# Row numbers carried in the sorted rows instead of looked up by table products: a recurrence and a hash-routed mixture of experts on one core

## The chip, the cores and the metric

The kernel runs on one core of a Trainium2 chip. The metric is the device time of one execution in microseconds. Three timed executions of the kernel before took 664.62, 650.76 and 662.44 us; their median, 662.44 us, is the time before. The profile page and the trace come from a further execution, with the profiler, which took 499.46 us. Times within the kernel are read from that execution, and the median of the timed executions is what is predicted.

The engines are called TensorE (PE in the profile; PEld is its loading of weights), VectorE (DVE), ScalarE (ACT), GpSimd (POOL) and SyncE (SP). An entry such as SPq is the queue of an engine's sequencer, here one that issues transfers.

## The reference

Two stages follow one another: a gated recurrence over the sequence and a mixture of experts in which each token goes to the one expert that a hash of its token number names.

```python
batch, seq, d_model = (4, 5056, 256)          # x, f_logit: f32
N, D, E, F = (20224, 256, 8, 1024)            # experts' weights w1 [E, D, F], w2 [E, F, D]: f32

# recurrence
sig = 1.0 / (1.0 + np.exp(-f_logit))
f = lower_bound[None, None, :] + (1.0 - lower_bound[None, None, :]) * sig
i = 1.0 - f
for t in range(S):
    h = f[:, t] * h + i[:, t] * x[:, t]
    y[:, t] = h

# experts, on y as rows [N, D]
expert_idx = token_ids * np.int64(2654435761) % np.int64(E)
for e in range(E):
    mask = expert_idx == e
    xe = x[mask]
    h = np.maximum(xe @ w1[e], 0.0)
    out[mask] = h @ w2[e]
```

The multiplier leaves the remainder 1 when divided by 8, so the expert is the low three bits of the token number. The kernel takes these and sorts by them.

## The kernel before

The sequence is cut into 25 blocks of 64 to 256 steps, each for all four batches; a "group" is 32 steps of four batches, so 128 tokens, and there are 158 of them. All work is cut into tasks, and a packed list (`ORDER`) fixes the order in which the engines get them.

A block is loaded, transposed so that time runs along the free axis, put through the sigmoid and the gate (on ScalarE or VectorE, as the order says), scanned by VectorE, and transposed back into rows. In the first seven blocks TensorE transposes; in the others VectorE does.

Each token gets a place: its rank within its expert, found with running sums and small matrix products. GpSimd then writes a group's 128 rows of y to their places in a sorted array in HBM, with one indirect transfer a group:

```python
srt = dram.tile([E * CAP, D], BF16, name="srt")          # 8 experts x 21 tiles x 128 rows
...
def scatter_rows(k, m, ybuf):
    bi = nc.gpsimd.indirect_dma_start(
        out=srt[:], out_offset=bass.IndirectOffsetOnAxis(ap=pos_i[:, G0[k] + m:G0[k] + m + 1], axis=0),
        in_=T["yT", k][:, m, :], in_offset=None, bounds_check=E * CAP - 1, oob_is_err=False,
    )
```

In seven blocks (`FS`), four of the eight groups go another way. They are sorted by expert on the chip with one-hot matrices and matrix products, written to a scratch array, and moved as one segment of 104 rows for each expert:

```python
def onehot(g=g):
    for c in range(4):
        nc.vector.tensor_scalar(oneh[:, c, :], iotf[:], qf[:, g, c:c + 1], None, op0=ALU.is_equal)
def sort(v, k=k, g=g):
    ...
    nc.tensor.matmul(t[:, j, :], lhsT=oneh[:, c, (2 * v + j) * P:(2 * v + j + 1) * P], rhs=T["yT", k][:, 4 + c, :], ...)
def put(g=g, queue=queue):
    queue.dma_start(scr[g % 3][:4 * P, :]..., T["sb", g]...)
def move(h, k=k, g=g, queue=queue):
    for e in range(4 * h, 4 * h + 4):
        bi = queue.dma_start(srt[bass.ds(T["reg", g][E + e], SEG), :], scr[g % 3][bass.ds(T["reg", g][e], SEG), :])
```

A tile of 128 sorted rows (there are 21 for each of the 8 experts, 168 in all) can be used when all blocks that may reach it have been written. It is read transposed, multiplied by w1, passed through Relu, and multiplied by w2. Its rows go out to their tokens' places by an indirect transfer:

```python
def read(j=j, e=e):
    xe = mp.tile([P, 2, P], BF16, name="xe", bufs=8)
    r0 = e * CAP + j * P
    bi = nc.sync.dma_start_transpose(xe[:], srt[r0:r0 + P, :])
def up(j=j, e=e):
    for f in range(FF):                                   # FF = 8
        for h in range(2):
            nc.tensor.matmul(hp[:, f, :], lhsT=w1_sb[e][:, h, f * P:(f + 1) * P], rhs=xe[:, h, :], ...)
def relu(eng, j=j, e=e):                                  # ScalarE or VectorE
    ...
def down(j=j, e=e, n=n, h=h):
    for f in range(FF):
        nc.tensor.matmul(op[:, h, :], lhsT=T["hT", j, e][:, f, :], rhs=w2_sb[e][:, f, :], ...)
def rows(j=j, e=e, n=n, h=h):
    bi = nc.gpsimd.indirect_dma_start(out=out, out_offset=bass.IndirectOffsetOnAxis(ap=row_i[:, c:c + 1], axis=0), ...)
```

For the last step the kernel must know which token lies in each sorted row (`row_i`). It finds out by products, block by block: one-hots of a token's place within its tile (A) are multiplied by one-hots of its tile, scaled by the two halves of its row number (BP), and summed into a table:

```python
nc.vector.tensor_tensor(A[:, c0:c1, :], iota_lo[...], lo_h[...], op=ALU.is_equal)
nc.vector.tensor_tensor(hi, iota_hi[...], hi_h[...], op=ALU.is_equal)
nc.vector.tensor_tensor(BP[:, c0:c1, 0, :W], hi, v1[...], op=ALU.mult)
nc.vector.tensor_tensor(hi, hi, v2[...], op=ALU.mult)
...
nc.tensor.matmul(tp[:, :, :W], lhsT=A[:, c, :], rhs=BP[:, c, :, :W], ...)
...
nc.vector.tensor_tensor(t, t, T["tp", k][:, :, :W], op=ALU.add)
```

The experts' weights are loaded as f32 on SyncE's queue into the buffers of x and f, and cast to bf16 by ScalarE or VectorE:

```python
nc.sync.dma_start(o.rearrange("k (h f) -> k h f", h=2), moe_w1[e].rearrange("(s h k) f -> k s h f", s=2, h=2))
...
if eng == "ACT":
    nc.scalar.copy(o, i_)
else:
    nc.vector.tensor_copy(o, i_)
```

A flag, computed from the data, leads to a second path for inputs whose tokens are spread too unevenly; the trace doesn't enter it.

Of the kernel before, what the change touches and what calls it, by code (L numbers as in the profile page):

```python
# [11 lines left out]
FP32 = mybir.dt.float32  # L12
BF16 = mybir.dt.bfloat16
FP16 = mybir.dt.float16
I32 = mybir.dt.int32
# [20 lines left out]
RANGES = [(0, 6), (6, GA), (GA, MID), (MID, NG)]  # L36
FILL = (9, 12)
FB = {GA: [9, 10, 11], MID: [13, 15, 17, 19]}
FS = [k for a in (GA, MID) for k in FB[a]]
GF = len(FS)  # L40
FA = ()
SEG = 104
XF = 3
OFF, TABD = 20.0, 25.0
W0, W1 = -70.0, 6.0
# [4 lines left out]
    "jrsgQ8_Q5CFiayEC?J+qP}nww06Q&U<6qwr$(CZCkrPQ5D9d;jAx<&ib(ttUnvTMzMj6u^4PH10z^8Glq?1;cTc`#A2~HEQJ}w5;J9nu#_ePi^+x"  # L50
    "=W8$*WY#Iy93}($Z=Ga&hfh}d8#b%4yc(aKuV-rjyGo7Vl6U`D9ku_zLSSquE5u3$kvQ;br+rnm><!mL}%qFu_EWJr>uCc9b8=GS?noMS{*=|;w5"
    "ZlM*u{9<eTWjXC?B)#H&knGgY=_Bg*0C&XI9tzlnxyQ4-^C8GgX}bG!LphgEQdL4j+k5QEW6Imv7=@;Yi91S^X3?9#s0B{tT{W*E|`1lE-"
    "T9}s+KH1tH3V%OFjv^Xr{6&DyQN661(anoAPEao5F50!7nq(ulZ-}zPau{u@@{JTfl0vimVQ+Z626%?4e1-"
    "DzTSr4?DpUvRdpj+rXZ)jg0YEtS)<PzAzOeH(%LRc7@erCm96aSY_6cRbv=@HyPm(tIvLztWd>tVqMrzb3;95#Ph%}_Qo_~Rn1#d0IIW0po5$Kma"
    "oAg@OLa5bT$o4HOLIvAq(VyH0C#J&Dycj@Sb%w4Owx>3;Cd%dCCexW0s3GVQpD5^M_S}LZQDbKjaK`XKhSGe%t3ZY0U>#7)n3~Qxe*<NW2V`f{(0"
    "7sHb_t%0ds;i&cg@svJ~@@}VlB$o#I4!lUuJPy-V2KBg+f;4yh`lY~d-v4W^Pc2E=I1i2s=Zv*LgvY-"
    "~^=5d3>JZX@J=i_;U{6PjDk0%e(^AthKpg_<9;`3s>9yEkZycEyF>O;YxI4{F9^2|Y&pe)a88bN8Eisyzxyc|!>%LmnXVO|lc^BO#B&=`tAXXwQ%"
    "1pS}^WaCYsCa)OO;w5-?-"
    "V|2wdwvx!3N7KjU(b8<D6Ax}9khbB(2iH)jd(uO4l46HL3e1v6Y>On4S%3I@Gj6A@|$9;6Yt0?K;57RbcHm$Jw!E4c|YDPc<76pw7fBI9&~{AydL"
    "iy^x-{W0B;fG<lUe@AH)Yi4&Dpu^OiwX-imh#R&vdX@`1b#^oG8?YcPvDJ~(L2&+<9^3NOM#yc<tphXk{EcRn;2&OIN;!*~Nep0DHQ`6WJ&&*kTM"  # L60
    "e^|{g@U{Gr4-Y2r`N1&WkT-`(d?FtVm-&cbWUwG;!w10RpeJ7#wB?KVD87MD2|n?w-"
    "0+RTR=zhF0*m?7U{i3B@8|o19{els1XcKEzKo|62l+tQ#((l3d>S9kuLU>x7hW5N!XchfSiY2h<_Gu~m;hV&bZ+6X5BP0<Jt)MQ!FRqqxWTsvhl3"
    "r#FgP9*U}O32;ApTj*cFW7xA<><Cm0Te%?y4w*b@{qkAf%a33uQjtC-"
    "1;1yA`i9tKPJbT|?`^CyDm+`w4)#h>~IK{!l=aqu_@!E9IrGvHn@9!9`7-Vr9j{ouL(6Z{RL*nfNuFfkJXco8gv%p#h|BBI(e{7tYJxSb4h;Z-"
    "1PU&tYr!^>bJEP>a-NRW0G#I-HNTG#=5Ai7uznZ!KECSItM9PA2M32|&Z5nm{~4q{j>NTAIr4#O%q#rwc<h-DMl(|i-O6jLCkZ6y-"
    "f(Qpp3i&3y1BG{cUU95(Lb_28)5p6pW+dd2~!Dg5b?_n=Qvb!L$%_Sn+oAA<qh9i(t?1NMyw=H6xKt8br?!s1h<x`6^VmGXTBK8EN6>UUbQP}3ON"
    "1>P~D$c_UQQ79VCn1?Q1`DBzZ7-^dx50jBD^5Xi+d=$-0ye3rCSI!xa2aNai!c=m+LE?}eF3-"
    "N3Y4~GY&kIvl8EYdJ0uq$_y_+FYT5&E6+ZHNP{?)^x8V-du=k;?K-"
    "S4Vg?IcVl(+ABDVtu@vK4Ixu?^n%3U;=51|MJnG!>`8*#}U`b`^)9v;7EjM1A`T=82i2i?{|~pn>RS8;Os8u6Pb7#Y2dQ4Mk&t*xmN9pVV;SZ5&L"
    "FA<@(Rh9=?@y!C_ZIQtbCzEi#IL5P82cE0!nLqt9C4c`0LKzK?F6=&g#A8bE+j>BwXd;@=>kBEdC1;)fP5N;QU>oCIJfXMhAjIAx=Vmg!<3wzszw"  # L70
    "yx+aPK!Ds0zQTkEFO-uOGIE}<0Dusnu&h4xman>i71!^SBw5O6ArL%AwEXMq?iIz;svqDrpI@{rL}9sKr7`L@e?xRc##u#+TG#@EVU)gL@_~p^%-"
    "!Log|XsGP_481WbVEMJoKJE{W8b3-e+YTyEFe+*lrq;0jwAOJF{nEH>J8mgGed9XHvrVzbDI(Xbv0SroJ4dYd1|h&=eiZxP>pNgOS<+C-"
    "QZ6Jj<@gS+fDJ4Kuoqr_CP*KW5P>@=aImIbgF7Q}tF6xPCA@~1D3`)xj18Y^HKtb&(qQ*4RZF$WgLE_lEe!m?NnE8-"
    "4Y39r~v=C=K%UfZkUosA%`iK^HEYvTz4vJU?C^|1j~!|V2lxMOeFx1ugK#GCe*xGPGtd*Y~gV&B-u)?q|h9h+fu?2k{yecK8TiWYcW^v2fs-sX`V"
    "v8ZW-"
    "4{amtiq8bf5B9n3gl(~m>5RkhrR|1?#7BF}zOa4pfgOp5#djOoMRMJ70QSWm*ijmsf_ddw9Ebr%ku~v=ePwIlC!1Twa{aI|dh9F*VQlwTM3r%50o"
    "erGV=tVKA&lmtyBYXHByzt*JNzkPxKa3948}ixD~`svvL}wiotVn~5f;CR;W!l&yYZOXC6SBqs|dp(I1SUv&teQFbu)1l4#hMwo=fKb`Ytk^3&#a"
    "G0Sn3muCVMR*I`VTUw#p@a5~P$g&5yW#0-wfIhfEDlF8j79D)DTBwT_iToLzA%$Dh06<5YB#f7q%<e`-"
    "A0CtnBaT#WG%W(}Bm+P^d+<<ejs4L;h%bs#AR+HOMgid1%S6yz$l5QjJ!m6&TEbEToWSocRv6rmjcHl}}f!8pz+>M*Cf-"
    "B{+$vW;J=8zBZ5O$Xm_TXMTif6FCtmv}KvzS$~&@rs*>dDgX9L|+B-"  # L80
    "C?ZcYPl>jlYEK|TxE9)Yr6~B+YNS&+;wc|F5(STp)GhE8@ul~)a8_y(7W5%Lq5Vj?j~Nw)^eD<gD3DY4tGP`GyH%d*H_-"
    "f=Ll*uwv=yhp8SoHTFHKLAMVEpAyilKEndMk@*~cX?c_Urf)PV8slWSy_i%uFfdgGs`h<}nOh!_t@Fg~tgIrtr2Y=#dXWU{LS%o{I_qag*#n0GWe"
    "!(RYLQQ1g#!5vP8sn@RCx0QqKh&f{Cvm(3dVtX=a%hBGB$qnpMmk3Kae_mNKoebbdW{ijuZu(p=oQAIB-BiP!}hX+oG-"
    "s(YMSI?({d?@Q$pJ6F3C|Y8>Oc!@~TWkQ79Kh30;=kWm1YkaVRn^b35b;nTBS`sG+zN4bsv|myEW#=`t~`ay#7tx!Pr*eQt^@NEzw6%uZ`v8A?t?"
    "DILY9{c@e#AWymql!Fes!!9>XmNVr|xn8bud1#|cL76BgMGqZvg=mw@OSj~0S(u8^9k<z4r+id|;?Zt*Lr#^~<SzHdWv1fv#FeEZt|FD7a<s+Wca"
    "7+-t4-zUnbfKV?QzZMxqRxT$x3ua-jna-dwEKxqB_);9=M0DBt3F9sWQ!wDe0?=5h|=|QI)W_j?`)S!hLWZDP|}uHKwz&F4dzit_PJ;&8Z1BrH}5"
    "L%TEO;3$>%~t~4E!=Vc4(L`P+N>O-I0OIM%H$-"
    "xv={cxk`mn%g*sWWw;mJ|yjsxXS6`chSjq8__eVbT06*NY6r^e1F=Us4UB<FX&6^VO&e^`;nVDE)NF{cCqo26RFGcHz{JrczfLL9u*m>Q6;f2LIW"
    "`_HleNAI~?S0W^^;#R(0gHq?z`hvJ6f`#Drhb*GeSG$mAyMp6Qm!VjW9auTKYOnJ(v#?S)VM45alUsR2yxPCG%r_6pD&85{eol^TOehPI}xqLh*q"
    "h^p&GsA{ci008knxy8_xUdo`kuR;%_(e33_R<PkOe<*{CGlmwR8!O%66y?XrnR(+mQYo{g|^dQSzN87w7$IJYAYS23cinuAIj>xtHge?YU-"  # L90
    "2vYQCJ$t!nsv)J^ROtFC6#`ml;VkIJj|(=0kfCn%r)Coj`Zs^n|>+P<f%><`d&T1MH_1bRfx{bAZgC#i=zMfufPYUUG!>iR2mk8-"
    "FZRLh^E({wfLJl&xBzJ<!E`l>I~OI7jXsh;0J4SYY}&@ZKzw3}M`w{)M5(nczvdaDaGRTWg%Xb&~^H|a4wpkvg?5AX>?x2UzhO@-"
    "7Cnx$URacbqWtJgH!_xE*t6F*3`@y<unZ|EUCp^J2v!u(V6{v9bjP+g*VDqJm5gFVwBb%%!d1%9ULq&ljvlnCBaB%L_)fi|kRI-&ka-"
    ")N}cthT7(D!Vp*lj^K~(RW&?rm1I?B*gV^`WQCCi*V49bz6nuUDQ?;_@tp>e*6FJ{s~*`r>itNijJ=1{ZC1JJ<2D8xju!SuVREp)noill|Z*s9aM"
    "XjNXOJOR7#y#@A8?o^&@>+ojjCJr_wLzGmZAK!ava>Ki1FjN%TKTr?cp#{y7!WCG|m7R_pM;lvOYD6V-"
    "B`LyuE6bbg&$?^XMKHl1F_);m;AolEagg>_>cK^F*5stf82x|FV>i|9i>j^3t9>vDR6I^fs%eZIav>?7(Fq1<}6U+s(PBmSr#uUhGhy1Y)NSNbx#"
    "ovx~r>mj;=_PUrZu2=YKx~8tB8|byZq3)_z`O`j=uC9;!COVHk<6G;VdVnsWD~6x&jdX3j&NtPkd>ehtkJIh-"
    "N#9I&2;ZQ(>9%^3&a2P*IyxnE*Xva!-BI__J#=q9Q1{WDbn4J~HB^V|LHeAktn2CK;WPCxJy@rKkY1sOhqurpw9$3-T-{kO(c^WhP#4`dJZ-"
    "3@9;qkmKyTI)!o&2G@b!A49;MTTX6e~_s-CBp>S=m@cz@kbkJjm7nVzFp>IHg(UZ|~J74Gydy<Bh6tMzo9A+%Ai(PQ=2@ELlO-lrGq-"
    "FlneulMLhdW=30zE`i++x0<xD14pXsdwlj`mp{F4ZxtQ"  # L100
# [54 lines left out]
def kernel(  # L155
# [19 lines left out]
    WMAX = 8 * max(window(k)[1] - window(k)[0] + 1 for k in range(NB))  # L175
# [10 lines left out]
    srt = dram.tile([E * CAP, D], BF16, name="srt")  # L186
    scr = [dram.tile([4 * P + SEG, D], BF16, name=f"scr{i}") for i in range(3)]
    i32a = consts.tile([P, NT], I32, name="i32a")
    iota_lo = consts.tile([P, P], BF16, name="iota_lo")
    iota_hi = consts.tile([P, NT], BF16, name="iota_hi")  # L190
# [8 lines left out]
    Tab = consts.tile([P, 2, NT], FP32, name="Tab")  # L199
# [17 lines left out]
    ids7 = rp.tile([P, GA], I32, name="ids7")  # L217
    tok = rp.tile([P, NH, 32], I64, name="tok")
    tlow = rp.tile([P, NH * 32], I32, name="tlow")
# [13 lines left out]
    nmax = rp.tile([1, 2], FP32, name="nmax")  # L233
    handt = rp.tile([P, 8, 4], FP32, name="handt")
    row_id = rp.tile([P, NG], I32, name="row_id")
    row_t = rp.tile([P, NG], I32, name="row_t")
    lowt = rp.tile([P, NG], FP32, name="lowt")
    hight = rp.tile([P, NG], FP32, name="hight")
    eb_all = rp.tile([P, NG], BF16, name="eb_all")
    v1 = rp.tile([P, NG], BF16, name="v1")  # L240
    v2 = rp.tile([P, NG], BF16, name="v2")
    lo_h = rp.tile([P, NG], BF16, name="lo_h")
    hi_h = rp.tile([P, NG], BF16, name="hi_h")
# [12 lines left out]
    pl.pool("xe", 8)  # L256
    pl.pool("hT", 3)
    pl.pool("ob", 4)
    pl.pool("tb", 1)
# [6 lines left out]
    def init_pool():  # L266
        make_identity(nc, idf[:])
        nc.gpsimd.iota(i32a[:], pattern=[[1, NT]], base=0, channel_multiplier=0)
        make_upper_triangular(nc, up1[:], diag=False)

    def init_pool1():
# [5 lines left out]
        nc.gpsimd.memset(m8[:, :, 0:1], 0.0)  # L277

    def init_pool2():
        nc.gpsimd.memset(Tab[:], 0.0)  # L280
        nc.gpsimd.iota(
            oneh.rearrange("p c s -> p (c s)").bitcast(I32)[:, 512:1024].rearrange("p (j q) -> p j q", j=4),
            pattern=[[1, 4], [4, P]], base=0, channel_multiplier=0,
# [30 lines left out]
    def init_dve2():  # L314
        nc.vector.tensor_copy(iota8[:], i32a[:, :E])
        nc.vector.tensor_scalar(up1[:], up1[:], -1.0, None, op0=ALU.add)
        nc.vector.tensor_copy(idn[:], idf[:])
# [1012 lines left out]
```

## Time and profile before

| what | value |
|---|---|
| timed executions, median (lowest, highest) | 662.44 us (650.76, 664.62) |
| profiled execution | 499.46 us, of which the core's span 497.7 us |
| mean granted TensorE clock | 0.906 |
| bytes moved by transfers | 106.21 MB in 116,035 packets, mean 213 GB/s |
| indirect transfers by GpSimd | 130 to the sorted array (mean 1052 ns), 168 to the output (mean 1028 ns) |
| transposing reads on SyncE's queue | 168, median 1196 ns of issue |
| up-products, down-products | 2688 of 128 columns, 1344 of 256 columns |
| casts of weights | 18 on ScalarE (18.5 us), 14 on VectorE (9.8 us) |

The page has these parts. The first gives the busy time of each engine and its share of the span. The second cuts the span into 40 slices, with tenths of busy time, of the TensorE clock and of the transfer engines' time. The chain that ended last follows the work back from the last instruction: at each step to what released it, or to the instruction before it on its engine. The groups table has one row for each kind of instruction: how many, busy time, mean, and the idle time ahead of them with its releasers. Of the waits, each row says which engine and line waited for what, with the sum in microseconds, the number of times and the longest.

A busy TensorE need not be working at its rate, because products are pipelined and their recorded durations overlap. For GpSimd the recorded span of a transfer is that of its issue, not of the movement of data.

### The profile page before, as it was taken

What the parts mean: (1) busy time and instruction counts of PE and PEld (TensorE: products, weight loads), DVE (VectorE), ACT (ScalarE), POOL (GpSimd) and SP (SyncE); (2) the same over time, 40 slices, a digit from 0 to 9 for tenths busy, and PEclk for the clock granted to TensorE, in tenths of its full rate; (3) what the DMA queues carried; (4) which work ended last, traced back from release to release, by engine and by line L of the source; (5) the groups of instructions that cost most, each with busy time, mean ns of one, the idle gap of its engine ahead of it and who ended that gap; (6) DMA issues with size and microseconds to landing.
All of it is one profiled execution on the core that took longest, in us unless ns stands there. A gap on an engine that the chain in (4) does not pass through costs nothing.

```text
span 497.7 us, 12978 instructions
## 1 busy us (share of the span) xinstructions
PE 389.5 (78%) x4690; PEld 350.0 (70%) x4690; DVE 391.3 (79%) x916; ACT 328.9 (66%) x475; POOL 320.9 (64%) x385
## 2 busy tenths in 40 slices
PE   3655557885686997866997889799869978899990
PEld 2544446774586887756896779689859868899980
DVE  2799746899999899949898969898897896854430
ACT  2479445788787888656997769687757564565430
POOL 8066162457775767737777577776657776777772
PEclk9756588998798999979999899999989989999996
DMA  8999999999799989897999799699747773454521
GB/s 212 375 369 379 296 298 346 307 311 244 189 229 207 218 210 238 211 211 184 193 223 216 184 195 231 128 205 213 216 139 179 208 165 102 142 144 125 149 98 45
DMA packets 116035, 106.21 MB, mean 213 GB/s; under 512 B 59953, under 2 KB 99869, under 8 KB 115967
## 3 DMA queue, kind: packets, MB, share of 16 engines
q1 hardware_dynamic: 101743, 76.04, 60.5%
q0 software_dynamic: 12352, 29.28, 23.3%
q8 instruction: 38, 0.62, 0.6%
q10 hardware_dynamic: 1872, 0.02, 0.2%
q14 instruction: 30, 0.25, 0.2%
HBM read 61.47 MB, written 37.09 MB: 198 GB/s over the span
## 4 chain that ended last, share of the span: by engine, by line
PE 38%; DMA 17%; DVE 6%; ACT 5%; issue 4%; POOL 2%; SPq 2%; POOLq 0%; DVEq 0%; ACTq 0%
PE hp L1168 19%; PE op L1186 16%; DMA xe<-srt 14%; ACT hT L1177 3%; PE so L1017 2%; POOL out_dram L1200 2%; DVE y L969 2%; DMA f_t<-in_f_logit_dram 1%; SPq L1158 1%; DVE xT L952 1%; DVE sT L926 1%; DMA srt<-yT,pos_i 1%; ACT sT L940 1%; DMA x_t<-in_x_dram 1%; DVE xT L926 1%
## 5 line engine op out<-in xcount | busy, mean ns | idle before, releaser
L1200 POOL DMA_INDIRECT out_dram<-ob,row_i x168 | 172.8, 1028 | 75.9 <-issue 43.6
L1168 PE MATMUL hp<-xe,w 128*128 128x128 bf16 x2688 | 181.1, 226 | 50.7 <-DMA xe<-srt 40.4
L1177 ACT ACTIVATE hT<-hp 128x1024 bf16<-128x1024 f32 x152 | 153.7, 1023 | 85.7 <-PE hp L1168 67.4
L1168 PEld LDWEIGHTS <-w 128*128 128x128 bf16 x2688 | 167.8, 101 | 60.2 <-DMA xe<-srt 32.9
L676 POOL DMA_INDIRECT srt<-yT,pos_i x130 | 136.7, 1052 | 90.5 <-issue 33.8
L1186 PE MATMUL op<-w,hT 128*128 128x256 bf16 x1344 | 177.8, 284 | 9.4 <-ACT hT L1177 5.5
L1186 PEld LDWEIGHTS <-hT 128*128 128x128 bf16 x1344 | 131.4, 102 | 29.6 <-ACT hT L1177 7.7
L969 DVE TENSOR_TENSOR_SCAN y<-sT,y,xT 128x256 bf16<-128x256 f32 (+2 forms) x128 | 78.4, 645 | 0.2
L940 ACT ACTIVATE sT<-sT,lb_c,c_c 128x256 f32<-128x256 f32 (+2 forms) x109 | 57.9, 566 | 6.8 <-DVE sT L926 6.7
L1194 ACT COPY ob<-op 128x512 f32<-128x512 f32 x68 | 39.1, 585 | 17.7 <-PE op L1186 15.5
L926 DVE STREAM_TRANSPOSE xT<-x_t 128x512 f32<-128x512 f32 (+1 forms) x64 | 38.6, 619 | 13.7 <-DMA x_t<-in_x_dram 11.8
L952 DVE SCALAR_TENSOR_TENSOR xT<-sT,xT 128x512 f32<-128x512 f32 x56 | 37.2, 675 | 15.4 <-ACT sT L940 15.1
L1179 DVE TENSOR_SCALAR hT<-hp 128x1024 bf16<-128x1024 f32 x16 | 19.5, 1221 | 28.7 <-PE hp L1168 24.6
L926 DVE STREAM_TRANSPOSE sT<-f_t 128x512 f32<-128x512 f32 (+1 forms) x64 | 38.0, 613 | 0.1
L899 ACT ACTIVATE f_t<-f_t 128x1024 f32<-128x1024 f32 (+1 forms) x29 | 29.6, 1027 | 6.5 <-DMA f_t<-in_f_logit_dram 4.9
L773 DVE TENSOR_TENSOR_SCAN y<-sT,y,xT 128x256 bf16<-128x256 f32 (+1 forms) x48 | 31.4, 691 | 0.3
L1093 DVE TENSOR_TENSOR A<-iota_lo,lo_h 128x512 bf16<-128x512 bf16 (+1 forms) x41 | 26.8, 653 | 0.9 <-PE tp L1110 0.9
L812 PE MATMUL yp<-idn,y 128*128 128x128 bf16 x88 | 12.6, 266 | 17.3 <-DVE y L773 10.5
L743 PE MATMUL tf<-idf,f_t 128*128 128x128 f32 x92 | 17.7, 339 | 9.6 <-DMA f_t<-in_f_logit_dram 7.0
L988 DVE STREAM_TRANSPOSE yT<-y 128x256 f32<-128x256 f32 (+2 forms) x68 | 22.8, 363 | 0.0
L812 PEld LDWEIGHTS <-y 128*128 128x128 bf16 x88 | 7.6, 115 | 21.0 <-DVE y L773 15.8
L752 ACT ACTIVATE sT<-sT,lb_col,c_col 128x256 f32<-128x256 f32 x39 | 21.7, 596 | 0.2
(142 smaller groups left out, 314.2 us busy)
## 6 DMA issues: line engine op xcount, KB each, us to landing
f_t<-in_f_logit_dram SPq DMA_DIRECT2D x50, 256.0 KB
x_t<-in_x_dram SPq DMA_DIRECT2D x50, 256.0 KB
f_t<-in_moe_w_dram SPq DMA_DIRECT2D x8, 1024.0 KB
x_t<-in_moe_w_dram SPq DMA_DIRECT2D x8, 1024.0 KB
f_t<-in_f_logit_dram SPq DMA_DIRECT2D x10, 512.0 KB
x_t<-in_x_dram SPq DMA_DIRECT2D x10, 512.0 KB
srt<-scr SPq DMA_DIRECT2D x56, 52.0 KB
xe<-srt SPq DMA_TRANSPOSE x168
```

What stands on the lines that cost most here:

```text
L676: bi = nc.gpsimd.indirect_dma_start(out=srt[:], out_offset=bass.IndirectOffsetOnAxis(ap=pos_i[:, G0[k] + m:G0[k] + m + 1], axis=0), in_=T[ ...
L773: nc.vector.tensor_tensor_scan(yv[:, h, b, :tt], T["sT", un][:, h, c], T["vT", un][:, h, c], init, op0=ALU.mult, op1=ALU.subtract,)
L899: nc.scalar.activation(v, v, AF.Sigmoid)
L926: nc.vector.transpose(o, i_)
L940: nc.scalar.activation(v, v, AF.Identity, scale=c_c[:, c:c + 1], bias=lb_c[:, c:c + 1])
L952: nc.vector.scalar_tensor_tensor(x_.rearrange("p s c l -> p (s c l)"), f_.rearrange("p s c l -> p (s c l)"), 1.0, x_.rearrange("p s c l -> ...
L969: nc.vector.tensor_tensor_scan(yv(T["y", k])[:, cp, :L, s], T["sT", k, u][:, s, n, :], T["xT", k, u][:, s, n, :], init, op0=ALU.mult, op1= ...
L1168: nc.tensor.matmul(hp[:, f, :], lhsT=w1_sb[e][:, h, f * P:(f + 1) * P], rhs=xe[:, h, :], start=(h == 0), stop=(h == 1),)
L1177: nc.scalar.activation(hT[:], T["hp", j, e][:], AF.Relu)
L1186: nc.tensor.matmul(op[:, h, :], lhsT=T["hT", j, e][:, f, :], rhs=w2_sb[e][:, f, :], start=(f == 0), stop=(f == FF - 1),)
L1194: nc.scalar.copy(ob[:], T["op", n // 2][:])
L1200: bi = nc.gpsimd.indirect_dma_start(out=out, out_offset=bass.IndirectOffsetOnAxis(ap=row_i[:, c:c + 1], axis=0), in_=T["ob", n // 2][:, h, ...
```

## The change

The change has five parts that go together.

1. **Row numbers travel with the rows.** A sorted row grows from 256 to 288 bf16 values; the added 32 hold the two halves of the token's row number, repeated. One small copy for each block writes them next to y, the sorted groups get them by small products, and one transfer for each tile number (21 in all, 8 experts at once) reads the two values of each row back. The table of one-hots and its products go away.
2. **Tiles are read in twos.** For 16 of the 21 tile numbers, two neighbouring tiles of the same expert are read by one transposing transfer, and the up-products run over 256 columns. Five tile numbers stay single.
3. **Weights come by GpSimd.** Its transfers convert f32 to bf16 on the way, so nothing is cast afterwards and the buffers of x and f are not used for weights.
4. **Eleven sorted groups instead of seven.** Three of them are put and moved by ScalarE's queue instead of SyncE's.
5. **A new searched order** of all tasks, with 6 instead of 8 buffers for read tiles and 4 instead of 3 for the Relu's output.

The core of the diff; the packed order, ranks, flag and second path are cut:

```diff
-FILL = (9, 12)
-FB = {GA: [9, 10, 11], MID: [13, 15, 17, 19]}
+RA = 46
+RANGES = [(0, 6), (6, RA), (RA, MID), (MID, NG)]
+FILL = [(8, 11), (11, 13)]
+RW = 288
+FB = {RA: [9, 10], MID: list(range(12, 21))}
-FA = ()
+FA = (2, 5, 8)
+DUO = [(1, 2), (3, 4), (5, 6), (7, 8), (12, 13), (14, 15), (16, 17), (18, 19)]
+XE, HT = 6, 4
...
-    srt = dram.tile([E * CAP, D], BF16, name="srt")
+    srt = dram.tile([E * CAP, RW], BF16, name="srt")
...
+        if e in SW:                                      # all eight experts
+                    if v:
+                        nc.gpsimd.dma_start(w1_sb[e][:], moe_w1[e].rearrange("(s h k) f -> k s h f", s=2, h=2))
+                    else:
+                        nc.gpsimd.dma_start(w2_sb[e][:], moe_w2[e].rearrange("(q p) d -> p q d", p=P))
...
+    def id_cols(eng, k):
+        o = T["yT", k][:, :NGS[k], D:].rearrange("p m (r s) -> p m r s", s=2)
+        i_ = vv[:, G0[k]:G0[k] + NGS[k], None, :].to_broadcast((P, NGS[k], (RW - D) // 2, 2))
...
+        def sort_ids(k=k, g=g):
+                    nc.tensor.matmul(
+                        t[:, j, :], lhsT=oneh[:, c, j * P:(j + 1) * P], rhs=T["yT", k][:, 4 + c, D:D + 2],
...
-            nc.vector.tensor_tensor(
-                A[:, c0:c1, :], iota_lo[:, None, :].to_broadcast((P, n, P)),
-                lo_h[:, gs, None].to_broadcast((P, n, P)), op=ALU.is_equal,
-            )
-            ...                                          # BP, the products into tp, the sums into Tab
+                bi = nc.sync.dma_start(
+                    row_v[:, j, :, :], srt.rearrange("(e c) d -> c e d", e=E)[j * P:(j + 1) * P, :, D:D + 2]
+                )
+            nc.vector.scalar_tensor_tensor(
+                pi[:], row_v[:, j, :, 1], 256.0, row_v[:, j, :, 0], op0=ALU.mult, op1=ALU.add
...
-            bi = nc.sync.dma_start_transpose(xe[:], srt[r0:r0 + P, :])
+            bi = nc.sync.dma_start_transpose(xe[:, :, :w], srt[r0:r0 + w, :D])     # w = 128 or 256
...
-                        hp[:, f, :], lhsT=w1_sb[e][:, h, f * P:(f + 1) * P], rhs=xe[:, h, :],
+                        hp[:, n * w:(n + 1) * w], lhsT=w1_sb[e][:, h, f * P:(f + 1) * P], rhs=rhs()[:, h, :],
```

Counted in the instruction lists of the two kernels: 64 transposing reads of 256 rows and 40 of 128 instead of 168 of 128; 114 indirect transfers to the sorted array instead of 130; 88 segment moves instead of 56; 176 sorting products instead of 112, and 176 more of two columns; 1024 up-products of 256 columns and 640 of 128 instead of 2688 of 128. Between ScalarE and VectorE the order moves work: 30 Relu evictions on VectorE instead of 16, 73 gates instead of 34, 11 evictions of sorted rows instead of 1.

## The prediction

> **What bounds the kernel now.** I read the busy table first, then the forty slices, the chain that ended last, and the stages in steps of 50 us.
>
> ```profile
> PE 389.5 (78%) x4690; PEld 350.0 (70%) x4690; DVE 391.3 (79%) x916; ACT 328.9 (66%) x475; POOL 320.9 (64%) x385
> PEclk9756588998798999979999899999989989999996
> DMA  8999999999799989897999799699747773454521
> PE 38%; DMA 17%; DVE 6%; ACT 5%; issue 4%; POOL 2%; SPq 2%; POOLq 0%; DVEq 0%; ACTq 0%
> ```
>
> No engine is full over the span, and the chain gives TensorE only 38% by its matmuls; 17% of it is transfers. The stages show where engines fill (columns: stage, its length, busy PE, PEld, DVE, ACT, POOL, clock, DMA share, GB/s):
>
> ```profile
> 0.00:50.00 50.00, 25.88 (x178) 21.75 (x178) 36.77 (x110) 29.55 (x48) 26.86 (x101) 0.72 1.00 334
> 100.00:150.00 50.00, 36.91 (x449) 33.35 (x447) 49.07 (x131) 40.58 (x69) 35.95 (x35) 0.90 0.97 243
> 300.00:350.00 50.00, 45.71 (x595) 42.15 (x593) 44.96 (x98) 40.27 (x57) 36.92 (x35) 0.97 0.92 193
> 450.00:498.00 48.00, 34.79 (x464) 32.36 (x461) 15.61 (x34) 15.34 (x19) 29.29 (x30) 0.91 0.35 101
> ```
>
> First VectorE: 49.07 of 50 us in the third stage, where the recurrence, the tables and the ranks share it. Then everything at once: PE 45.7, VectorE 45.0, DMA share 0.92. At the end only PE and GpSimd still matter. The waits name what TensorE lacks, and the table of groups the cost of one:
>
> ```profile
> PE hp L1168 <- DMA xe<-srt: 40.4, 21, 4.7
> POOL out_dram L1200 <- issue: 43.6, 136, 2.0
> L1177 ACT ACTIVATE hT<-hp 128x1024 bf16<-128x1024 f32 x152 | 153.7, 1023 | 85.7 <-PE hp L1168 67.4 <-issue 8.2 <-PE op L1186 7.6
> L1093 DVE TENSOR_TENSOR A<-iota_lo,lo_h 128x512 bf16<-128x512 bf16 (+1 forms) x41 | 26.8, 653 | 0.9 <-PE tp L1110 0.9
> ```
>
> So TensorE stops 21 times, 40.4 us in all, for a transposing read of sorted rows. ScalarE mostly waits for TensorE and is not the bound. The table line is one of the costs that the change strikes out.
>
> A busy TensorE is not one at its peak, so I take the floor from the chain in order of time: 32 up-products in 1.79 us (56 ns) and 8 down-products in 0.87 us (109 ns). A tile is 16 × 56 + 8 × 109 = 1.77 us; 168 tiles make **297 us**. The rest, from the cadence of the timeline (last start less first, over the count): 184 f32 transposes at 0.11 = 20, 112 sorting products at 0.109 = 12, 158 table products at 0.025 = 4, small ones 8. Together about 341 us of 497.7.
>
> The other floors. GpSimd: each indirect transfer is 0.97 us plus a gap of 0.30 us, so (130 + 168) × 1.27 = 378 us. The gap is the "issue" wait above. SyncE's queue: 168 transposing reads × 1.20 = 202, 164 loads × 0.57 = 93, 56 segment moves × 0.79 = 44, the rest 24: 363 us. VectorE: 391 us. These are four floors between 341 and 391; the span is what the dependence between them adds.
>
> **The Trainium skill.** "TensorE: Matmul & The Clock Gate", section "Back-to-back issue gap", gives N/2.4 + 2.5 ns for a warm array: 55.8 ns at N = 128 and 109.2 at 256. The trace agrees (56 and 109). The same section warns of about 81 ns per N = 128 product in a stream with weight loads; this trace doesn't show that in the chain, which matters below. "DMA: Bandwidth & Descriptors", section "Issuing engines are not separate DMA queues", says that all issuers share the same 16 DMA engines and that another issuer only saves sequencer time. I apply it to the weights; the trace before has no weight load from GpSimd to compare. That page's "Rules for kernel authors" says that small transfers should be coalesced; the 4-byte row numbers go the other way, and no run so far shows their price.
>
> **The change, part by part.**
>
> *Tables out.* On VectorE: A 26.8, three BP passes 10.7 + 11.2 + 11.2, sums into Tab 4.6, splitting ranks into high and low about 4, two iotas 0.4: −69 us. TensorE −4.
>
> *Row numbers in.* Copies into 25 blocks' rows, 14 on VectorE and 10 or 11 on ScalarE at about 0.3 (estimate from the short copies): +4 and +3; 21 pairs of small operations instead of 19: nothing. SyncE: 21 reads × about 0.6 (a load's issue) = +13. DMA: 21 × 128 × 8 = 21,504 pieces of 4 bytes on top of 116,035 packets; rows 12.5% longer.
>
> *Weights by GpSimd.* Casts go: VectorE −9.8 (6.4 + 3.4), ScalarE −18.5 (11.2 + 7.3). SyncE −9. GpSimd +16 × (0.9 + 0.3) = +19, taking 0.9 from the plain load of the lower bound, the nearest thing in the trace. All 16 lie in the first stretch, among the first scatters.
>
> *Eleven sorted groups.* Four more groups save 16 scatters: GpSimd −20. They cost TensorE 64 × 0.109 = +7 and 176 two-column products of some 0.04 = +7, VectorE 16 × 0.365 = +6 of one-hots, four more evictions, and 32 moves (24 of them issued by ScalarE): SyncE +6.
>
> *Tiles in twos.* 64 reads of 256 rows and 40 of 128 instead of 168. At 1.4 (estimate: the 1.20 of a single one and a little) and 1.2 this is 138 instead of 202: SyncE −64. The up-products become 1024 of 256 columns and 640 of 128: 1024 × 0.109 + 640 × 0.056 = 147.5 instead of 150.5. Halving the weight loads is worth **3 us only**, because the stream already ran at its column rate.
>
> *The order.* It also shifts work from ScalarE to VectorE: 14 more Relu evictions × 1.22 = +17, gates 34 to 73 (+39, mostly at 0.36) = +13, eviction of sorted rows 10 × 0.7 = +7, small ones +4.
>
> Sums: VectorE 391 − 79 + 51 = **364**; ScalarE 329 − 18.5 (casts) − 14 (Relu) − 39 × 0.57 (gates) − 5 (evictions) + 4 (row numbers) = 274; SyncE 363 − 54 = **309**; GpSimd 378 + 19 − 20 = **377**; TensorE 341 + 7 = **348**.
>
> So no work leaves TensorE or GpSimd. The gain has to come from VectorE in the stages where it is 80 to 98% busy, and from a shorter SyncE queue in front of the reads for which TensorE waits. I count VectorE's 27 us in full, since they leave the middle stages, and a fifth to a quarter of the 40.4 us of read waits, 8 us. 497.7 − 35 = **463 us** in the profiled execution, a ratio of 0.93.
>
> **From the profile to the timed runs.** The profiled execution took 499.46 us and the three timed ones 650.76 to 664.62. No view explains the 163 us between them. I carry the ratio over: 662.44 × 0.93 = 616, and take **615**. If the extra time is a fixed addition, it is 463 + 163 = 626; if the changed kernel's timed runs come out at its profile's level, 465. That, not the engines, makes the range wide.
>
> **Rivals.**
> 1. *DMA becomes the bound.* For it: share 0.91 to 1.07 up to 350 us; the change adds 21,504 tiny pieces and about 5 MB (filling 1.4, moves 2.3, scratch writes 1.4). Against: the same share carries 334 GB/s in the first stage and 193 later, so it is rather occupancy than a limit on bytes. If true, reads land later, TensorE's wait rises over 60 us, and the time stays within 2%, 650 to 675.
> 2. *GpSimd becomes the bound.* For it: 377 us of issue against a span of 463, sixteen weight loads ahead of scatters, and a tail already made of it: TensorE ends at 475 us, the last output issue at 488. If the order leaves gaps, 640.
> 3. *VectorE's relief goes into waiting.* The scan waits for gates and loads as before, and TensorE's order ends at the same time: 655.
> 4. *Better than I count*: reads of two tiles feed TensorE without stops, nearly all 40 us go; profile 440, timed 585.
>
> **Range and chances.** With 465 (timed runs at the profile's level) at one in five, 585 to 640 at one in two, and rivals 1 and 3 for most of the rest, I take 468 to 665. Faster by over 2% 0.78, within 2% 0.11, slower 0.11; slower mainly by rival 1 or by weights arriving late for the first tiles.
>
> **What would show each step.** VectorE near 364 us and ScalarE near 274 confirm the sums; VectorE well under 45 of 50 in the stages from 100 to 350 us confirms the relief. TensorE's floor unchanged shows in the same cadences, 109 ns at 256 columns. The wait of up-products for reads should fall from 40.4 to about 30; over 60 means rival 1, also seen as GB/s falling at a share near 1. A chain with long stretches of output issues means rival 2. The row-number reads should not appear among the waits. I would be wrong if a casting load holds GpSimd far longer than 0.9 us, if TensorE's early stretch waits for weights, or if timed and profiled times of the changed kernel are related in another way than before.

## The result and the profile after

| executions | before | after | ratio, 95% interval |
|---|---|---|---|
| timed together, median (lowest, highest) | 657.78 us (650.76, 664.62) | 617.57 us (615.08, 627.18) | 0.9438 [0.9358, 0.9518] |
| profiled, mean TensorE clock | 499.46 us, 0.906 | 616.63 us, 0.827 | not to be compared |

The changed kernel is 5.6% faster, 615 us was predicted, and yet its profile is 117 us longer than the one the prediction started from. One fact of the runs is needed to read all that follows: the same kernel took about 501 us on one chip (called A here) and 664 to 669 us on three others (B, C, D), the first timings were taken at the level of these three, and every ratio below compares kernels on one chip. Each of the four was used in one session only, so "chip" may also stand for what else differed between the sessions. The profile of the kernel before that the prediction worked with has the level of chip A. Some ratios are given a second time as "like for like": they compare the mean of those executions alone that lie within 1.5% of the fastest of their kernel in that session. For the table above this is 0.946.

The busy table, the clock and transfer lines of the slices and the chain of the changed kernel's page, for the lines shown of before:

```profile
PE 436.7 (71%) x3750; PEld 356.3 (58%) x3750; DVE 376.7 (61%) x810; ACT 280.1 (46%) x410; POOL 315.5 (51%) x384
PEclk9766766757987897879789968889678978897998
DMA  8958899999998798299864565657286624542321
PE 44%; issue 16%; DMA 11%; another core or an unknown queue 8%; ACT 7%; POOL 6%; DVE 3%; SPq 3%; POOLq 0%; ACTq 0%; DVEq 0%
```

No engine is over 71%, and the transfer engines are near full only in the first half. ("Another core or an unknown queue" is what the profile writes where it finds no releaser that it knows; the kernel uses one core.) "Issue", time in which an engine waited for nothing that the profile shows, has grown from 4% to 16% of the chain. The clock line has more low tenths; the mean is 0.827 instead of 0.906. The stages (columns as before):

```profile
0.00:50.00 50.00, 24.91 (x169) 20.76 (x170) 30.95 (x78) 19.62 (x37) 17.63 (x46) 0.83 0.84 243
100.00:150.00 50.00, 27.70 (x223) 22.65 (x223) 36.34 (x99) 22.39 (x36) 26.85 (x27) 0.67 1.25 205
300.00:350.00 50.00, 41.15 (x406) 33.66 (x405) 33.76 (x65) 30.83 (x44) 22.43 (x22) 0.96 0.56 150
450.00:500.00 50.00, 39.25 (x298) 30.21 (x296) 29.85 (x64) 18.39 (x25) 27.63 (x28) 0.81 0.62 151
```

In none of these stages is an engine full; the share of the transfer engines is highest from 100 to 150 us (1.25). The waits of TensorE, of its weight loads and of GpSimd (columns: sum in us, times, longest) show where time stands still:

```profile
PE hp L1203 <- issue: 21.2, 26, 7.0
PE hp L1203 <- DMA xe<-srt: 7.4, 3, 6.6
PEld L1203 <- issue: 81.0, 50, 9.5
PEld L1220 <- issue: 26.0, 26, 6.7
POOL out_dram L1234 <- ACT ob L1228: 133.9, 33, 10.0
```

The reads, 40.4 us of waiting in the old profile, are down to 7.4; in their place the weight loads of the up-products stand still 50 times, 81.0 us, and the profile shows nothing that they wait for. To know what of this is the change and what is the chip, a profile of the kernel before at the same level was needed. One experiment gives it in all but the weights: weights by GpSimd in the kernel before, on chip B. The waits of that kernel:

```profile
PE hp L1156 <- issue: 68.0, 74, 8.6
PE hp L1156 <- DMA xe<-srt: 9.0, 1, 9.0
PEld L1156 <- issue: 113.2, 113, 9.1
PEld L1174 <- issue: 38.1, 37, 8.0
```

And the kernel before, unchanged, on chip A:

```profile
PE hp L1168 <- DMA xe<-srt: 35.7, 20, 4.0
PEld L1168 <- issue: 23.6, 19, 4.1
```

So the waits for reads (35.7 us on chip A, 9.0 on chip B) nearly vanish on the slower chip, and "issue" takes their place. These two kernels differ in how the weights come; a kernel that was run at both levels without any difference (the kernel before without its tables, below) shows the same, with 50.0 us of such waits on chip A and on chip D:

```profile
PE hp L1125 <- DMA xe<-srt: 11.6, 6, 3.7
```

Summed over all rows of TensorE's matmuls and weight loads (the two overlap), "issue" is 40 us for the kernel before on chip A, 274 for the one on chip B, and 191 in the changed kernel's profile; for the kernel without tables it is 34 us on chip A and 290 on chip D.

What such a wait looks like, in the timeline of TensorE and of SyncE's queue of the changed kernel (start, duration, what, idle time before it):

```profile
426.22 0.27 PE L733 MATMUL so<-yT,oneh 128*128 128x256 bf16 x1 [0.46 <-issue]
426.93 0.27 PE L733 MATMUL so<-yT,oneh 128*128 128x256 bf16 x1 [0.44 <-issue]
427.66 0.27 PE L733 MATMUL so<-yT,oneh 128*128 128x256 bf16 x1 [0.46 <-issue]
```

```profile
427.58 6.39 SPq L784 DMA_DIRECT2D srt<-scr  x4
```

Four such moves in the profile before:

```profile
200.09 3.15 SPq L1052 DMA_DIRECT2D srt<-scr  x4
```

Sorting products that otherwise follow each other at 109 ns start 0.71 and 0.73 us apart, although nothing in the profile holds them; in the same stretch four segment moves take 6.39 us on SyncE's queue instead of 3.15. The instructions of VectorE and ScalarE aren't longer: the mean of the scan is 646 ns on chip A and 645 on chip B, the mean Relu on ScalarE 1022 and 1025.

One more table serves all experiments: when the first, a tenth, half and all of the down-products had started, counted in the traces (us).

| kernel, chip | first | 10% | 50% | last |
|---|---|---|---|---|
| before, A | 60 | 141 | 307 | 488 |
| changed, up-products cut in two, A | 112 | 169 | 333 | 500 |
| before with weights by GpSimd, B | 64 | 166 | 398 | 654 |
| changed, B | 109 | 168 | 385 | 613 |
| changed, weights first, B | 132 | 189 | 406 | 638 |
| changed, C | 109 | 167 | 376 | 615 |
| changed, up-products cut in two, C | 109 | 168 | 397 | 632 |

### The profile page after: what moved, and what is told of

Same layout as the page of the kernel before. It is cut to its first block, busy times and chain, and to the rows that moved or that the text cites. A ratio compares the mean times of both kernels' runs of the same rounds, so it can differ in the third digit from the quotient of the medians.

```text
span 614.9 us, 10965 instructions
## 1 busy us (share of the span) xinstructions
PE 436.7 (71%) x3750; PEld 356.3 (58%) x3750; DVE 376.7 (61%) x810; ACT 280.1 (46%) x410; POOL 315.5 (51%) x384
## 4 chain that ended last, share of the span: by engine, by line
PE 44%; issue 16%; DMA 11%; another core or an unknown queue 8%; ACT 7%; POOL 6%; DVE 3%; SPq 3%; POOLq 0%; ACTq 0%; DVEq 0%
PE hp L1203 21%; PE op L1220 19%; POOL srt L709 4%; ACT hT L1212 4%; PE so L733 3%; DMA srt<-yT,pos_i 3%; DMA w<-in_moe_w_dram 2%; DMA idt<-in_moe_token_ids_dram 2%; DMA xe<-srt 2%; DMA x_t<-in_x_dram 1%; DMA f_t<-in_f_logit_dram 1%; ACT f_t L1035 1%; DVE y L902 1%; SPq L1193 1%
## 5 line engine op out<-in xcount | busy, mean ns | idle before, releaser
L1234 POOL DMA_INDIRECT out_dram<-ob,row_i x168 | 171.3, 1020 | 207.4 <-ACT ob L1228 133.9
L1203 PE MATMUL hp<-xe,w 128*128 128x256 bf16 (+1 forms) x1664 | 201.1, 273 | 77.5 <-ACT hT L1212 37.6
L1203 PEld LDWEIGHTS <-w 128*128 128x128 bf16 x1664 | 152.3, 106 | 110.5 <-issue 81.0
L1220 PE MATMUL op<-w,hT 128*128 128x256 bf16 x1344 | 192.7, 294 | 27.3 <-issue 16.4
L709 POOL DMA_INDIRECT srt<-yT,pos_i x114 | 119.2, 1045 | 84.7 <-issue 31.4
L1214 DVE TENSOR_SCALAR hT<-hp 128x1024 bf16<-128x1024 f32 x30 | 36.4, 1219 | 70.9 <-remote 29.9
L1076 ACT ACTIVATE sT<-sT,lb_c,c_c 128x256 f32<-128x256 f32 (+2 forms) x77 | 40.4, 557 | 2.0 <-DVE yT L957 2.0
L733 PE MATMUL so<-yT,oneh 128*128 128x256 bf16 x176 | 29.1, 295 | 13.7 <-issue 13.7
L876 ACT ACTIVATE sT<-tf 128x512 f32<-128x512 f32 x23 | 13.7, 596 | 48.1 <-DVE y L902 34.7
L733 PEld LDWEIGHTS <-oneh 128*128 128x128 bf16 x176 | 17.5, 104 | 19.7 <-issue 17.1
L872 PE MATMUL tx<-idf,x_t 128*128 128x128 f32 x92 | 21.5, 381 | 10.1 <-DVE xT L887 4.7
```

Of the source, the lines that this page charges most:

```text
L709: bi = nc.gpsimd.indirect_dma_start(out=srt[:], out_offset=bass.IndirectOffsetOnAxis(ap=pos_i[:, G0[k] + m:G0[k] + m + 1], axis=0), in_=T[ ...
L872: nc.tensor.transpose(view(t[:, h, :]), T[which, k][:, u * nch + n, h * P:(h + 1) * P], idf[:])
L1076: nc.scalar.activation(v, v, AF.Identity, scale=c_c[:, c:c + 1], bias=lb_c[:, c:c + 1])
L1203: nc.tensor.matmul(hp[:, n * w:(n + 1) * w], lhsT=w1_sb[e][:, h, f * P:(f + 1) * P], rhs=rhs()[:, h, :], start=(h == 0), stop=(h == 1),)
L1220: nc.tensor.matmul(T["op", n][:, h, :], lhsT=lhs(f), rhs=w2_sb[e][:, f, :], start=(f == 0), stop=(f == FF - 1),)
```

## The experiments

The theories. *A*: where TensorE and SyncE's queue are held up between instructions, the time follows the number of instructions fed to them. *B*, the prediction's: relief of VectorE and fewer waits for reads. *C*: on a chip without holding up the change gains nothing. *D*: the 4-byte row numbers cost time. *E*: the first tiles wait for weights, so that earlier loads help. *F*: scatters wait behind the loads in GpSimd's queue, so that earlier loads hurt.

**The kernel before once more (chip A).** No edit.

> The kernel before, unchanged, for a second profile. The trace after shows stretches in which TensorE and SyncE's queue advance by one instruction every 0.7 us (a register MOVE takes 687 ns there instead of 29), and the first trace before (499 us) shows none. Theory A (these stretches make the usual time): a profile of an ordinary execution near 655 us shows them too, with over 60 us of TensorE waiting for issue, against 35 us in the first trace. Rival B (the prediction: engine work and read waits): the profile is the first one stretched, with read waits well over 40 us and no such stretches. Time 645 to 670 in both.

501.76 us beside 501.28 for the other executions of it, ratio 1.0013 [0.9988, 1.0038]. So 501 us is the level of this chip, and the old profile's 499.46 is no outlier of the profiler. Both theories had 645 to 670 us here, and both missed. The expectations of the next three runs are times of the slower level too, so that only their differences can be held against what chip A shows.

**The 256-column up-products cut in two (chip A).** It has 1,024 products and 1,024 weight loads more than the changed kernel, and all else of the change.

```diff
-    for h in range(2):
-        ...
-        hp[:, n * w:(n + 1) * w], lhsT=w1_sb[e][:, h, f * P:(f + 1) * P], rhs=rhs()[:, h, :],
+    for c in range(0, w, P):
+        for h in range(2):
+            ...
+            hp[:, n * w + c:n * w + c + P], lhsT=w1_sb[e][:, h, f * P:(f + 1) * P], rhs=rhs()[:, h, c:c + P],
```

> The changed kernel, but its 1024 up-products of 256 columns are made as 2048 of 128, with as many weight loads: 1024 products and 1024 weight loads more on TensorE, all else the same. Theory A (time follows the number of instructions that TensorE must be fed): 635 to 660 us, most of the gain over the kernel before lost. Rival B (column rate): 2 to 6 us more than the changed kernel's 618, so 619 to 625.

509.18 us, ratio to the kernel before 1.0172 [1.0080, 1.0265]. With VectorE 16 us and ScalarE 48 us less busy than before (374.7 and 280.8 against 391 and 329), it isn't faster here but slower. The wait for reads:

```profile
PE hp L1204 <- DMA xe<-srt: 33.7, 15, 5.8
```

33.7 us against 35.7: with reads in twos, and with the new order and two buffers fewer for read tiles, it is hardly shorter. The stages of the two kernels on this chip, first the kernel before, show where it loses and regains:

```profile
100.00:150.00 50.00, 38.20 (x450) 34.63 (x448) 49.14 (x130) 40.70 (x69) 36.23 (x36) 0.86 0.96 238
450.00:500.00 50.00, 38.15 (x517) 35.61 (x514) 16.95 (x40) 17.22 (x22) 31.06 (x32) 0.90 0.36 105
```

```profile
100.00:150.00 50.00, 31.68 (x351) 28.95 (x351) 40.66 (x108) 28.88 (x44) 28.80 (x29) 0.74 1.21 216
450.00:500.00 50.00, 49.54 (x656) 46.34 (x653) 25.72 (x50) 20.01 (x28) 36.35 (x38) 1.00 0.50 125
```

A tenth of the down-products is reached 28 us later (169 against 141); from there to the last it takes 331 us instead of 347, with TensorE full at the end (49.54 of 50 us). The later start costs more than the rate brings. What starts it later no run on this chip separates; in the stage from 100 to 150 us the transfer engines' share is 1.21 instead of 0.96.

**Half as many TensorE instructions for the experts, same columns (chip A).** Each product takes twice as many columns, and half of the weights' rows are left out, so the output is another one.

```diff
-        hp[:, n * w:(n + 1) * w], lhsT=w1_sb[e][:, h, f * P:(f + 1) * P], rhs=rhs()[:, h, :],
+        hp[:, n * w:(n + 2) * w], lhsT=w1_sb[e][:, h, fs[n] * P:(fs[n] + 1) * P], rhs=rhs()[:, :, :],
...
-    for f in range(FF):
+    for f in range(0, FF, 2):
...                                              # likewise twice as wide in the down-products
```

> The changed kernel with the same columns streamed by TensorE in half the instructions: up-products and down-products twice as wide, 1504 fewer products and 1504 fewer weight loads. It leaves out half of the weights (each product uses only every second chunk, and halves of the model width are mixed), so its output is not the reference's. Theory A: 3008 instructions fewer give 540 to 585 us. Rival B: columns and waits unchanged, 605 to 620.

495.34 us, 0.9878 [0.9811, 0.9946]. The trace lists 7,960 instructions against 13,013 of the cut kernel, and the two are 13.8 us apart: 2.7 ns for each. On this chip the number of instructions hardly counts: theory A had set the cut and the wide form 50 to 120 us apart.

**The kernel before without its tables (chip A).** It leaves out the one-hots A and BP, their products and the sums, and the splitting of ranks ahead of them; rows go to fixed row numbers instead of the computed ones.

```diff
-        nc.gpsimd.memset(Tab[:], 0.0)
+        nc.gpsimd.iota(row_i[:, :158], pattern=[[1, 158]], base=0, channel_multiplier=158)
...
-        def tb(c0, c1, k=k, jlo=jlo, W=W):
-            ...                                  # A, BP; likewise the products and the sums
+        def tb(c0, c1):
+            return
```

> The kernel before with the tables left out: no one-hots, no table products, no sums, and row numbers from a fixed pattern, so the rows go to wrong places; scatters and reads stay. VectorE loses some 69 us, TensorE 316 instructions. Rival B (the prediction's step: VectorE's relief in the middle stages counts in full): 25 to 40 us less than before, 615 to 632. Theory A (instructions): a few per cent of TensorE's instructions, 5 to 12 us less, 645 to 652.

497.23 us, 0.9924 [0.9895, 0.9953]. VectorE is busy 64 us less (327.1), and 4 us of it arrive. The waits say where the rest went:

```profile
PE hp L1125 <- DMA xe<-srt: 50.0, 25, 4.6
DVE xT L944 <- ACT sT L932: 39.5, 14, 8.5
```

TensorE now waits 50.0 us for reads instead of 35.7, and VectorE 39.5 us for ScalarE's gates instead of 16.4. The relief turned into waiting. The prediction's step had expected 25 to 40 us less.

**The changed kernel once more (chip B).** No edit.

> The changed kernel, unchanged, beside the kernel before in the same session. In the last runs the kernel before took 501 us and the split form of the changed kernel 509 us, without the stretches of one instruction every 0.7 us. Theory C (the gain of 5.6% came through those stretches: the changed kernel has 10965 instructions in its trace against 12978, and loses less to them; where there are none, it gains nothing): 498 to 506 us where the kernel before takes 501. Rival B (the prediction's ratio of 0.93 holds for the engines' work): 463 to 475 us.

623.67 us beside 668.00, ratio 0.9282 [0.9225, 0.9339]; like for like it is 0.938 (620.84 to 661.97 us). The gain is confirmed; the question of chip A wasn't answered, since this was another chip.

**Row-number reads doubled (chip B).** Each of the 21 transfers of 4-byte pieces is issued twice, first into a spare buffer.

```diff
-    nc.sync.nop()
-        ...
-        bi = nc.sync.dma_start(row_v[:, j, :, :], srt.rearrange(...)[j * P:(j + 1) * P, :, D:D + 2])
+    for dst in (row_w, row_v):
+        nc.sync.nop()
+            ...
+            bi = nc.sync.dma_start(dst[:, j, :, :], srt.rearrange(...)[j * P:(j + 1) * P, :, D:D + 2])
```

> The changed kernel with each of the 21 reads of row numbers made twice, the first into a second buffer that nothing uses: 21,504 more pieces of 4 bytes, 16 us of all transfer engines' time by the 13 ns that a piece takes in the trace after, and 21 more issues on SyncE's queue (0.6 us each). Theory D (transfers are near their limit up to 350 us, and the small pieces eat part of the gain): 5 to 12 us more than the changed kernel. Rival: they lie beside other work, 0 to 3 us more.

627.73 us, 0.9298 [0.9211, 0.9384], which can't be told from the changed kernel's 0.9282. By the ratios another 21,504 pieces cost 1 us, by the medians 4, and the intervals leave room for some 8 (estimate from both). Theory D's 5 to 12 us is not seen, but its low end isn't excluded.

**All weights ahead of the first scatter (chip B).**

```diff
-        return out
+        lw = [t for t in out if t.name.startswith("lw")]
+        out = [t for t in out if not t.name.startswith("lw")]
+        at = max(n for n, t in enumerate(out) if t.name in ("ip", "ip1", "ids4", "ids5", "ids6")) + 1
+        return out[:at] + lw + out[at:]
```

> The changed kernel with all 16 weight loads moved to the front of GpSimd's order, ahead of the first scatter (issued from 11 to about 30 us instead of 11 to 166 us). Theory E (TensorE's late start, first down-product at 108 us against 61 before, waits for weights): 8 to 20 us less than the changed kernel. Rival F (weights and scatters share GpSimd's ring in order, so scatters land behind the weights): 5 to 25 us more.

647.58 us, 0.9654 [0.9587, 0.9721]: 24 us more than the changed kernel (25 like for like), more than half of its gain. Its waits in the early part:

```profile
DVE yT L707 <- DMA srt<-yT,pos_i: 25.5, 1, 25.5
PE tf L875 <- ACT yT L958: 25.5, 3, 24.7
```

VectorE waits once, 25.5 us, for a buffer that a scatter is still reading, and TensorE waits behind that chain. The scatters go out on GpSimd's queue, now behind 16 loads of weights: the first goes out at 63 us instead of 42. The first down-product moves from 109 to 132 us, the last from 613 to 638: a late start is carried to the end, and of E and F it is F that holds.

**The kernel before with weights by GpSimd (chip B).** The sixteen loads convert on the way, the 32 casts go; nothing else is changed.

```diff
-                nc.sync.dma_start(o.rearrange("k (h f) -> k h f", h=2), moe_w1[e].rearrange(...))
+                nc.gpsimd.dma_start(w1_sb[e][:], moe_w1[e].rearrange("(s h k) f -> k s h f", s=2, h=2))
...
-            if eng == "ACT":
-                nc.scalar.copy(o, i_)
-            else:
-                nc.vector.tensor_copy(o, i_)
+            return
```

> The kernel before with one part of the change: weights loaded and converted by GpSimd's transfers at their places in the old order (10 to 74 us), no casts on ScalarE and VectorE, nothing else changed. The prediction's step: VectorE -9.8, ScalarE -18.5, GpSimd +19 us, worth 0 to 10 us less than before. Rival F (scatters land behind weights in the ring): 5 to 20 us more than before.

666.98 us, 0.9991 [0.9935, 1.0046]. This part alone is worth nothing that the interval, 4 us to either side, can show. Taking ScalarE's 18.5 and VectorE's 9.8 us of casts away did not bring the end forward. The 5 to 20 us of theory F don't show either, where the loads lie among the scatters.

**The changed kernel and the cut up-products side by side (chip C).** The edits are those above.

> The changed kernel, unchanged, once more beside the kernel before. Theory C (the gain comes only where TensorE and SyncE's queue are held up between instructions; without that, the later start of the experts eats the gain): where the kernel before takes about 501 us, this one takes 498 to 506 us, ratio 0.995 to 1.01. Rival B (the prediction's 8 us of read waits and 27 us of VectorE count everywhere): 463 to 475 us there, ratio 0.925 to 0.95. Where the kernel before takes 655 to 670 us, both say 615 to 630 us, ratio 0.93 to 0.945.

> The changed kernel with each 256-column up-product cut into two of 128 columns, as the kernel before has them: 1,024 products and 1,024 weight loads more, the rest as changed. Theory A (where the engine is held up between instructions, the time follows the number of instructions fed to TensorE): where the kernel before takes 655 to 670 us, this one takes 640 to 665 us, 20 to 40 us more than the changed kernel, so that most of the gain is gone. Theory B (the gain is VectorE's work and the reads): within 10 us of the changed kernel, 615 to 635 us. Where the kernel before takes about 501 us: 509 us again, and 3 to 10 us above the changed kernel by either theory.

625.63 us, 0.9391 [0.9292, 0.9490], and 643.35 us, 0.9652 [0.9552, 0.9752], beside 663.97 for the kernel before. Cutting the wide products takes back 17.7 of 38.3 us. The trace reaches a tenth of the down-products at the same time (167 and 168 us) and the last at 615 and 632: the whole difference is in the rate. The waits for "issue" at the up-products, first of the cut kernel:

```profile
PEld L1204 <- issue: 78.6, 88, 5.7
PE hp L1204 <- issue: 42.0, 63, 2.0
```

```profile
PEld L1203 <- issue: 75.8, 47, 8.7
PE hp L1203 <- issue: 20.2, 28, 3.7
```

The second fence is the uncut kernel on this chip: its up-products stand 28 times for "issue", the cut ones 63 times, 42.0 us instead of 20.2. The weight loads stand nearly twice as often (88 times instead of 47), but for about as long in all (78.6 and 75.8 us). Theory A said 640 to 665, B 615 to 635; A is right in kind, at the low edge in size.

**Without tables, and with half the instructions, on a slower chip (chip D).** The edits are those above, and so is what they leave out.

> The kernel before without its table products, without their eviction on VectorE and without the additions behind them (rows then go to fixed row numbers), once more. It takes 64 us of busy time off VectorE, and some 550 of 13,000 instructions, few of them TensorE's large ones. The prediction's step (VectorE's relief counts where it ends waits): 625 to 645 us where the kernel before takes 655 to 670 us. Theory A (instructions fed to TensorE decide there): 648 to 662 us, within 2% of the kernel before. Where the kernel before takes about 501 us: 497 us again.

> The changed kernel with about half as many TensorE instructions for the experts' products and the same number of columns (it leaves out half of the weights' rows), once more. Theory A: where the kernel before takes 655 to 670 us, this one takes 520 to 585 us, 40 to 100 us less than the changed kernel, although TensorE works through as many columns. Theory B (engine work and reads): 600 to 630 us there, as the columns, the evictions and the reads are those of the changed kernel. Where the kernel before takes about 501 us: 495 us again.

658.88 us, 0.9846 [0.9784, 0.9908], and 602.14 us, 0.9052 [0.8958, 0.9147], beside 668.91; like for like 0.989 and 0.910. Without the tables 7 to 10 us are won, as A said (648 to 662) and B (625 to 645) didn't. Half the instructions: A said 520 to 585, B 600 to 630. Here A's strong form falls, and B's range holds. The changed kernel wasn't timed on this chip; beside its like-for-like ratios of 0.938 to 0.946 elsewhere the gain is 18 to 24 us for some 3,000 instructions, 6 to 8 ns each (estimate across chips); the cut on chip C gives 17.7 us over 2,048, or 8.6 ns. At 8 ns the 9,380 matmuls and weight loads of the kernel before would account for 75 us, less than half of the 165 us between the chips. The number of instructions has a price there, but it isn't the whole of the slower level.

No run that does the whole computation was faster than the changed kernel.

## Why the prediction was right, and where it wasn't

The number was right and most of its reasons were wrong.

*Busy sums: nearly right.* VectorE was to come to 364 us and came to 376.7, ScalarE to 274 and came to 280.1. A weight load took 0.74 or 0.97 us of GpSimd where 0.9 was taken. The median transposing read took 1.20 us of SyncE's queue, 104 of both sizes together, where 1.4 was guessed for the double one; in the sums, which my medians undercounted, the reads came from 222 to 150 us. On the rate, 2,202 starts of weight loads in the changed kernel's trace follow the one before by 100 to 115 ns, which is the 109.2 ns that the formula for a single product in the Trainium skill's "TensorE: Matmul & The Clock Gate", section "Back-to-back issue gap", gives for 256 columns.

*One line misread.* For rival 2 I wrote that TensorE ends at 475 us. That is where the chain leaves it; the last down-product of that trace starts at 485 us, three microseconds ahead of the last output issue. GpSimd didn't become the bound of the whole: in the changed kernel it waits 133.9 us for rows that ScalarE has still to copy. Nor did the transfers in the sense of rival 1, for TensorE's wait for reads fell; that their share is high early (1.25 from 100 to 150 us) may belong to the later start, and no run separates it.

*VectorE's 27 us counted in full: failed.* The run without tables takes 64 us from VectorE and gains 4 us on chip A, 7 to 10 on chip D. Rival 3, relief that goes into waiting, described it; I had it at a low chance. The sign I had named for it, VectorE well under 45 us in the middle stages, was no test: at the slower level VectorE is low there before the change too (29 to 40 us in each of these stages in the kernel before with weights by GpSimd).

*8 us of read waits: failed.* On chip A the kernels with reads in twos still wait 33.7 and, with half the instructions, 30.8 us, against 35.7. At the level that was timed these waits hardly existed before the change (9.0 us on chip B).

*"3 us only" for half as many up-products: the term that was most mis-sized.* It is 17.7 us on chip C. I worked from the column rate, which is right for the stream, and the profile that I had came from a level at which an instruction has next to no price beyond it (2.7 ns on chip A).

*Weights by GpSimd: right that this part brings no gain by itself* (0.9991 alone). The Trainium skill's "DMA: Bandwidth & Descriptors", section "Issuing engines are not separate DMA queues", says that another issuer saves sequencer time only, and the run agrees. What I hadn't put into the sum was that scatters queue behind the loads: GpSimd's queue is in the path of the start, 24 us when all loads come first. In the changed kernel's chain up to 180 us the scatters are 14.7%, their landings 8.8% and those of the weights 8.4%. TensorE also waits 10.6 us for weights there, a sign of being wrong that I had named; earlier loads aren't the cure.

*Row numbers: right* that they don't show among the waits. These runs resolve no price for leaving the rule of that page's "Rules for kernel authors" that small transfers be coalesced; up to some 8 us stay possible.

*The ratio carried from the profile to the timed runs: right by luck.* The 163 us that no view explained are the distance between the two levels, at both of which the unchanged kernel was seen. At the profile's own level the prediction's step said 463 to 465 us. The changed kernel itself wasn't timed there, but the cut kernel (509.18) and the one with fewer instructions (495.34) lie on both sides of it; taking 2.7 ns for each of 2,048 instructions off the former, it is at some 504 us (estimate), level with the kernel before. So theory C is likely and not shown.

Where the 38 to 44 us (35 to 41 like for like) come from, then, on the slower chips: about 18 from wider up-products (shown on chip C), 7 to 10 from the tables (chip D, measured by leaving them out of the kernel before), none that shows from the weights (chip B). Some 10 to 17 us are left for reads in twos, eleven groups, the order and its buffers, less what the later start costs; this is a difference of runs on several chips, and no run separates these parts.

It stays open what holds up TensorE and SyncE between instructions at the slower level. The stretches follow the last 16 KB packet of the instruction queues in the trace by anything from under 1 to over 20 us, so no link shows. Nor is the lower clock set apart: the granted clock is either full or half in these traces, and half for 86 to 115 us of a run on chip A, for 188 to 240 us on the other chips. It may follow from the pauses or add to them. It doesn't explain the cut up-products, with 206 us of half clock before the cut and 214 after it on chip C.

## What to carry to other kernels

Before working out a gain, compare the profiled time with the timed ones; where they differ as here (499 against 662 us), the waits of the profile may not be those of the timed runs, and a second profile at the timed level tells more than sums from the first. Where "issue" is a large wait, try fewer and wider instructions even if the column rate says that they bring next to nothing (3 us by the rate, 17.7 us measured). Relief of a busy engine can turn into waits elsewhere (64 us less on VectorE, 4 us gained), and loads on a queue that also carries the scatters of the start cost less between them than ahead of them (24 us here).

## What was not expected of the hardware

- The same kernel with the same data takes 501 us on one chip and 664 to 669 on three others, at a mean TensorE clock of 0.887 to 0.920 on chip A and 0.804 to 0.846 on the others. The durations of VectorE's scans and ScalarE's Relu are the same within 3 ns on chips A and B.
- On the slower ones TensorE's matmuls and SyncE's queue at times advance by one instruction in about 0.72 us; the traces of chip A show next to none of it (weight loads that start 0.64 to 0.80 us after the one before: 7 in the kernel before, 70 on chip B, there with weights by GpSimd).
- TensorE's busy time grows there at unchanged columns, from 395.9 us (chip A) to 452.5 (chip C) for the cut kernel, whose clock is granted at half for 110 and 214 us.
